# Turning x by the DMA crossbar and placing side work by a table, in a fused attention and maxout kernel

## Chip, cores, metric

One core of one Trainium2 chip. The metric is device microseconds of one execution. A ratio is the mean time of one kernel's fast runs over the mean of the other's fast runs of the same rounds, so it isn't quite the ratio of the medians quoted beside it.

## The reference

Eight batches, eight heads, 576 tokens of 64 numbers. Keys and values are pooled by eight, the softmax attention's output is x (4608 tokens of 512), and a maxout layer follows:

```python
k_p = k.reshape(B, H, Sp, pool, D).mean(axis=3)          # Sp = 72
v_p = v.reshape(B, H, Sp, pool, D).mean(axis=3)
attn = softmax(scale * q @ k_p.T)
x = (attn @ v_p).transpose(0, 2, 1, 3).reshape(B * S, H * D)
h = np.maximum(np.maximum(x @ w1, x @ w2), x @ w3)       # 512 -> 768
out = h @ w_out                                          # 768 -> 512
```

Inputs and output are float32.

## The kernel before

The maxout layer works on blocks of 512 tokens, nine in all. A block has 18 slots of four matmuls `pw` (blocks 0 and 1 do the first half of them in half-size pieces, 27 slots in all) and four slots of six matmuls `po`. While block n runs, the attention of batch n+1 is done between the slots. A batch is 576 tokens, so a block starts 64 tokens further ahead of its batch each time: block 3 needs chunks 0 to 2 of batch 3, block 7 only chunk 0 of batch 7.

The attention gives x with tokens on partitions; the layer needs features there. So each chunk of 128 tokens is turned, by four TensorE transposes into PSUM and a copy:

```python
def turn_x(b, c0, keep, xn, tag, evac=nc.scalar.copy):
    pxt = psp.tile([128, KCH, 128], F16, name="pxt", tag=tag[0], bufs=tag[1])
    for kc in range(KCH):                                 # KCH = 4
        nc.tensor.transpose(pxt[:, kc, :],
            xn[:, kc // 2, 2 * (kc % 2):2 * (kc % 2) + 2, :], identh)
    g0 = S * b + c0
    evac(out=xT[:, :, g0 + keep:g0 + 128], in_=pxt[:, :, keep:128])

TR = ("tr", 1)        # one PSUM buffer for turning q, k and x
```

Side work came from generators, at slots given by a list of counts; loads were issued by GpSimd, each behind the fold (pooling by adds) that freed its buffer:

```python
PLAN = (2, 4, 5, 6, 8, 8, 9, 10, 11, 12, 13, 14, 15, 16, 17, 18, 18, 19, 19, 20,
        20, 21)
for n in range(1, TOK // NB):
    if n + 2 < B:
        fold_k(n + 2, nc.gpsimd)
        if n + 3 < B:
            load_k(n + 3, nc.gpsimd)
        fold_v(n + 2)
        if n + 3 < B:
            load_v(n + 3, nc.gpsimd)
            load_q(n + 3)
    ...                                   # cut: slots of the block, next(nxt)
```

Stores of the output go out on SyncE's queue (all but two small ones at the end).

The softmax here doesn't subtract the row's maximum and nothing guards it: scores larger than these inputs give would overflow.

Of the kernel before, what the change touches and what calls it, by code (L numbers as in the profile page):

```python
# [14 lines left out]
def kernel(  # L15
# [11 lines left out]
    nc = tc.nc  # L27
# [124 lines left out]
    def turn_q(b, n0, n1, evac, tag):  # L152
        if b not in qTs:
            qTs[b] = sb2.tile([128, 2 * NG, 128], BF16, name="qT", tag="qT")
        pqt = psp.tile([128, n1 - n0, 128], BF16, name="pqt", tag=tag[0],
                       bufs=tag[1])
        qf = qbs[b].rearrange("p hp t d -> p (hp t d)")
        for n in range(n0, n1):
            nc.tensor.transpose(pqt[:, n - n0, :], qf[:, 128 * n:128 * n + 128],  # L159
                                ident)  # L160
        evac(out=qTs[b][:, n0:n1, :], in_=pqt)  # L161
# [13 lines left out]
    def turn_k(b):  # L175
        pkt = keys(b, TR)
        for par in range(2):
            fill_kz(b, par, 0, H, pkt, nc.vector.tensor_copy)
# [22 lines left out]
    def new_et(b):  # L201
        ets[b] = sb2.tile([Sp, H, S], F16, name="et", tag="et")

    def scores(b, h):
        psc = psp.tile([128, 1024], F32, name="psc", tag="att", bufs=2)
        score(b, h, psc[:, 0:320], 0, 0, 5)
        score(b, h, psc[:, 320:512], 1, 0, 3)
        score(b, h, psc[:, 512:576], 1, 3, 4)
        exp(ets[b][:, h, :], psc[0:Sp, 0:S])

    def turn_x(b, c0, keep, xn, tag, evac=nc.scalar.copy):
        pxt = psp.tile([128, KCH, 128], F16, name="pxt", tag=tag[0], bufs=tag[1])
        for kc in range(KCH):
            nc.tensor.transpose(  # L214
                pxt[:, kc, :],
# [4 lines that stand above are left out]
    def values(b, c0):  # L220
        pav = psp.tile([128, 2, 512], F32, name="pav", tag="att", bufs=2)
        for h in range(H):
            nc.tensor.matmul(  # L223
                pav[:, h // 4, 65 * (h % 4):65 * (h % 4) + 65],
                ets[b][:, h, c0:c0 + 128], vp_all[:, b, h, :],
                start=True, stop=True)
        pv = pav[:, :, 0:260].rearrange("p g (h e) -> p g h e", e=65)
        rcp = sb3.tile([128, 2, 4], F32, name="rcp", tag="rcp")
        nc.vector.reciprocal(out=rcp, in_=pv[:, :, :, 64])  # L229
        xn = sb3.tile([128, 2, 4, D], F16, name="xn", tag="xn")  # L230
        nc.vector.tensor_tensor(  # L231
            out=xn, in0=pv[:, :, :, 0:D],
            in1=rcp.to_broadcast([128, 2, 4, D]), op=ALU.mult)
        return xn
# [2 lines left out]
    TR = ("tr", 1)  # L237
    PW = ("pw", 3)

    def queries(b):  # L240

        new_et(b)
        for m, (n0, n1) in enumerate(((0, 5), (5, 10), (10, 14), (14, 18))):
            turn_q(b, n0, n1, nc.scalar.copy, TR)
            yield
            if m == (3 if b == 2 else 2):
                turn_k(b)
                yield
        for h in range(H):
            scores(b, h)  # L250
            yield

    def outputs(b, order="v0 v1 x0 v2 x1 v3 x2 v4 x3 x4", tag=TR, evac=nc.scalar.copy):


        xns = {}
        for step in order.split():
            i = int(step[1])
            c0, keep = CHUNKS[i]
            if step[0] == "v":  # L260
                xns[i] = values(b, c0)
            else:
                turn_x(b, c0, keep, xns[i], tag, evac)
            yield

    def hidden_part(n, jc, c0, c1, hT):
        col = slice(NB * n + c0, NB * n + c1)
        t = None
        for wi in range(3):
            pw = psp.tile([128, c1 - c0], F32, name=f"pw{wi}", tag="pw", bufs=3)  # L270
            for kc in range(KCH):
                nc.tensor.matmul(pw, w_sb[wi][:, kc, bass.ts(jc, 128)],  # L272
                                 xT[:, kc, col],
                                 start=(kc == 0), stop=(kc == KCH - 1))
            if wi == 0:
                t = sb2.tile([128, c1 - c0], F16, name="t0", tag="t0")
                nc.scalar.copy(out=t, in_=pw)  # L277
            elif wi == 1:
                t1 = sb2.tile([128, c1 - c0], F16, name="t1", tag="t1")
                nc.vector.tensor_tensor(out=t1, in0=t, in1=pw, op=ALU.max)  # L280
                t = t1
            else:
                nc.vector.tensor_tensor(out=hT[:, jc, c0:c1], in0=t, in1=pw,  # L283
                                        op=ALU.max)
            yield

    def hidden(n, hT):

        halves = n < 2
        if halves:  # L290
            for c0 in (0, NB // 2):
                for jc in range(3):
                    yield from hidden_part(n, jc, c0, c0 + NB // 2, hT)
        for jc in range(3 if halves else 0, JCH):
            yield from hidden_part(n, jc, 0, NB, hT)
# [22 lines left out]
    def new_hT():  # L318
        return sb2.tile([128, JCH, NB], F16, name="hT", tag="hT")
# [4 lines left out]
    def heat(n):  # L324
        for _ in range(n):
# [3 lines left out]
    ATT = ("att", 2)  # L329
    new_kp(0)  # L330
    k16 = const.tile([96, 6, 4, D], F16, name="k16", tag="k16")
    pkp0 = [psp.tile([128, 6, D], F32, name="pkp", tag="pw", bufs=3)
            for _ in range(2)]
    heat(10)

    def add_k0(i):
# [1 line left out]
                                in1=kts[0][:, i:i + 2, 4:8], op=ALU.add)  # L338

    def sum_k0(i):  # L340
        for p in pkp0:
            for j in range(4):
                nc.tensor.matmul(p[:, i:i + 2], identh[0:96, :], k16[:, i:i + 2, j, :],
                                 start=(j == 0), stop=(j == 3))

    def put_k0(i, j):
        nc.vector.tensor_copy(out=kps[0][:, i:j, 0, :], in_=pkp0[0][0:96, i:j])
        nc.scalar.copy(out=kps[0][:, i:j, 1, :], in_=pkp0[1][0:96, i:j])

    add_k0(0)  # L350
    sum_k0(0)
# [45 lines left out]


    nc.vector.memset(kz_all[1], 0.0)
    hT0 = new_hT()  # L400
    out0 = outputs(0, "v2 v3 x2 v4 x3 x4")

    def early():
        pool_k(1, PW)
        yield
        turn_k(1)
        yield
        new_et(1)
        for m, (n0, n1) in enumerate(((0, 5), (5, 10), (10, 14), (14, 18))):
            turn_q(1, n0, n1, nc.vector.tensor_copy, TR)  # L410
            if m > 1:
                scores(1, m - 2)
            yield
        for h in range(2, H, 2):
            scores(1, h)
            scores(1, h + 1)
            yield

    side = early()
    steps = {18: 1, 19: 1, 21: 1, 22: 1, 23: 1, 24: 1, 25: 1, 26: 1}  # L420
    for slot, _ in enumerate(hidden(0, hT0)):
        if slot > 0:
            next(out0, None)
        for _ in range(steps.get(slot, 0)):
            next(side)
        if slot > 24:
            h = 4 * (slot - 25)
            pool_v(1, h, h + 4, TR, nc.scalar.copy)
    out1 = outputs(1, "v0 v1 x0 x1 v2 v3 x2 v4 x3 x4", evac=nc.vector.tensor_copy)
    for mm, _ in enumerate(project(0, hT0)):  # L430
        for _ in range((1, 0, 0, 0)[mm]):
            next(side)
        for _ in range((0, 1, 2, 2)[mm]):
            next(out1)
    side = out1
    fold_k(2, nc.gpsimd)
    load_k(3, nc.gpsimd)
    load_q(3)
# [1 line left out]
    load_v(3, nc.gpsimd)  # L440


    def batch(b):
        yield from queries(b)
        yield from outputs(b, *(("v0 v1 x0 v2 x1 x2 v3 x3 v4 x4",) if b == 2 else ()))


    PLAN = (2, 4, 5, 6, 8, 8, 9, 10, 11, 12, 13, 14, 15, 16, 17, 18, 18, 19, 19, 20,
            20, 21)
    PLAN1 = (9, 11, 13, 15, 19, 20, 21, 22, 23, 24, 25, 26, 26, 27, 28, 28, 29, 29, 30,  # L450
             30)
    for n in range(1, TOK // NB):
        if n + 2 < B:
            fold_k(n + 2, nc.gpsimd)
            if n + 3 < B:
                load_k(n + 3, nc.gpsimd)
            fold_v(n + 2)
            if n + 3 < B:
                load_v(n + 3, nc.gpsimd)
                load_q(n + 3)  # L460
        hT = new_hT()
        nxt = batch(n + 1) if n + 1 < B else iter(())
        plan = PLAN1 if n == 1 else PLAN
        slot = 0
        for part in (hidden(n, hT), project(n, hT)):
            for _ in part:
                if slot < 8:
                    next(side, None)
                for _ in range(plan.count(slot)):
                    next(nxt, None)  # L470
                slot += 1
        side = nxt


# [28 lines left out]
```

## Time and profile before

| | before |
|---|---|
| time, median of 4 | 264.33 us (264.19 to 265.34) |
| span of the profiled run | 262.3 us |
| TensorE / VectorE / ScalarE / GpSimd busy | 95 / 51 / 48 / 45 % |
| steady block (108.21 to 135.03 us) | 26.82 us |

TensorE is the bound, at full clock. In the timeline of an engine each row is a start, a length and a group of instructions; a bracket gives the idle time before it and what ended it. The prediction shows the lines, and how they are read.

```profile
L314 SPq DMA_DIRECT2D out_dram<-osb x5: 467/594/1353, 105.7 to 109.6; - x5
...
DMA to landing us min/median/max: 7.3/9.0/10.6
```

These five stores of 128 KB landed 7 to 11 us after issue, against a median of 2.4 over the kernel: v, q and k were being loaded just then.

### The profile page before, as it was taken

How to read it: one execution, taken by the hardware profiler on the slowest of the kernel's cores; microseconds unless marked ns; L12 is line 12 of the kernel's file. 1: busy time of each engine (PE TensorE's matmuls, PEld its weight loads, DVE VectorE, ACT ScalarE, POOL GpSimd, SP SyncE). 2: the span in 40 equal slices, each digit the busy share in tenths (PEclk: the TensorE clock that was granted, in tenths of full speed). 3: DMA queues.
4: the chain of work that ended last, by engine and by line, in shares of the span. 5: the costliest groups of instructions: out<-in, count | busy, mean ns of one | idle time of the engine just before them, and what ended most of it. 6: DMA issues, size and time to landing. Idle time of an engine off the chain costs nothing.

```text
span 262.3 us, 4747 instructions
## 1 busy us (share of the span) xinstructions
PE 250.3 (95%) x1902; PEld 142.6 (54%) x1902; DVE 132.7 (51%) x243; ACT 125.9 (48%) x225; POOL 117.6 (45%) x84
## 2 busy tenths in 40 slices
PE   7899999988997999999999999999999999999992
PEld 3678556675554555555555555555555554444441
DVE  4567561766344546364635463556446554523430
ACT  1464237243754574548464746464656463132221
POOL 8653000999899999899790896000000000000000
PEclk9999999999999999999999999999999999999998
DMA  7999999886698975987987705100510042015006
GB/s 185 202 197 209 199 234 226 257 202 113 157 238 180 196 182 115 231 266 139 215 239 180 113 4 132 28 2 0 121 42 0 2 110 50 4 41 119 0 12 152
DMA packets 21027, 34.73 MB, mean 132 GB/s; under 512 B 2668, under 2 KB 13548, under 8 KB 20428
## 3 DMA queue, kind: packets, MB, share of 16 engines
q0 software_dynamic: 14048, 21.44, 42.0%
q1 hardware_dynamic: 6796, 12.85, 19.3%
q8 instruction: 15, 0.25, 0.4%
q10 hardware_dynamic: 160, 0.13, 0.2%
q14 instruction: 8, 0.07, 0.1%
HBM read 34.60 MB, written 9.44 MB: 168 GB/s over the span
## 4 chain that ended last, share of the span: by engine, by line
PE 87%; DVE 4%; ACT 4%; issue 1%; DMA 1%; SPq 0%; DVEq 0%
PE pw L272 49%; PE po L305 16%; PE psc L194 6%; PE pav L223 4%; PE pqt L159 3%; PE pxt L214 3%; PE wm L326 2%; ACT xT L218 2%; PE pvp L148 1%; DVE t L280 1%; DMA out_dram<-osb 1%; ACT et L199 1%; DVE xn L231 1%; PE pkt L166 1%; DVE kz L171 1%
## 5 line engine op out<-in xcount | busy, mean ns | idle before, releaser
L272 PE MATMUL pw<-xT,mw 128*128 128x512 f16 (+1 forms) x720 | 158.1, 358 | 0.9 <-ACT xT L218 0.7
L272 PEld LDWEIGHTS <-mw 128*128 128x128 f16 x720 | 64.3, 98 | 48.5 <-issue 0.8
L280 DVE TENSOR_TENSOR t<-t,pw 128x512 f16<-128x512 f16 (+1 forms) x60 | 38.0, 633 | 75.2 <-PE pw L272 46.3
L277 ACT CAST t<-pw 128x512 f16<-128x512 f32 (+1 forms) x60 | 32.6, 543 | 41.6 <-PE pw L272 39.0
L305 PE MATMUL po<-mwo,hT 128*128 128x512 f16 (+1 forms) x222 | 51.5, 373 | 0.0
L199 ACT ACTIVATE et<-psc 72x576 f16<-72x576 f32 (+2 forms) x62 | 40.4, 661 | 16.1 <-PE psc L194 16.1
L283 DVE TENSOR_TENSOR hT<-t,pw 128x512 f16<-128x512 f16 (+1 forms) x60 | 37.9, 632 | 11.0 <-PE pw L272 7.8
L127 POOL TENSOR_TENSOR vt<-vt 72x2048 f32<-72x2048 f32 (+1 forms) x12 | 41.2, 3432 | 4.5 <-DMA vt<-in_v_dram 4.0
L127 POOL TENSOR_TENSOR kt<-kt 96x1536 f32<-96x1536 f32 (+1 forms) x12 | 31.5, 2622 | 23.2 <-DMA kt<-in_k_dram 22.6
L310 ACT COPY osb<-po 128x512 f32<-128x512 f32 (+1 forms) x36 | 20.8, 579 | 38.7 <-PE po L305 38.5
L305 PEld LDWEIGHTS <-hT 128*128 128x128 f16 x222 | 19.9, 97 | 19.4 <-DVE hT L283 1.7
L231 DVE TENSOR_TENSOR xn<-pav,rcp 128x512 f16<-128x512 f32 x40 | 27.6, 691 | 1.4
L194 PE MATMUL psc<-qT,kz 128*128 128x64 bf16 (+3 forms) x192 | 25.6, 246 | 1.2 <-DVE kz L171 1.2
L161 ACT COPY qT<-pqt 128x512 bf16<-128x512 bf16 (+1 forms) x25 | 15.9, 637 | 21.5 <-PE pqt L159 21.5
L194 PEld LDWEIGHTS <-kz 128*128 128x128 bf16 x192 | 17.5, 98 | 15.0 <-DVE kz L171 2.0
L218 ACT COPY xT<-pxt 128x512 f16<-128x512 f16 (+1 forms) x34 | 18.6, 547 | 4.3 <-PE pxt L214 4.2
L223 PEld LDWEIGHTS <-et 72*128 72x128 f16 x320 | 15.2, 98 | 4.6 <-issue 0.5
L223 PE MATMUL pav<-vp,et 72*128 72x65 f16 x320 | 17.2, 194 | 0.4 <-ACT et L199 0.4
L214 PEld LDWEIGHTS <-xn 128*128 128x128 f16 x160 | 11.7, 97 | 10.7 <-DVE xn L231 3.1
L229 DVE RECIPROCAL rcp<-pav 128x8 f32<-128x8 f32 x40 | 8.2, 204 | 18.4 <-PE pav L223 18.3
L214 PE MATMUL pxt<-identh,xn 128*128 128x128 f16 x160 | 15.5, 219 | 2.0 <-DVE xT L218 0.7
L159 PEld LDWEIGHTS <-qb 128*128 128x128 bf16 x144 | 10.0, 97 | 7.9 <-issue 2.4
(43 smaller groups left out, 116.8 us busy)
## 6 DMA issues: line engine op xcount, KB each, us to landing
out_dram<-osb SPq DMA_DIRECT2D x70, 128.0 KB, 2.4
kt<-in_k_dram POOLq DMA_DIRECT2D x5, 1152.0 KB, 8.3
vt<-in_v_dram POOLq DMA_DIRECT2D x5, 1152.0 KB, 10.0
qb<-in_q_dram POOLq DMA_DIRECT2D x7, 576.0 KB, 13.3
mw<-in_moe_w_dram POOLq DMA_DIRECT2D x9, 256.0 KB, 10.0
kt<-in_k_dram SPq DMA_DIRECT2D x3, 384.0 KB, 4.8
kt<-in_k_dram SPq DMA_DIRECT2D x1, 1152.0 KB, 10.0
vt<-in_v_dram SPq DMA_DIRECT2D x1, 1152.0 KB
```

The lines of the kernel that those rows point to most:

```text
L127: e.tensor_tensor(out=t[:, :, 0:n, :], in0=t[:, :, 0:n, :], in1=t[:, :, n:2 * n, :], op=ALU.add)
L194: nc.tensor.matmul(out, kz_all[b % 2][:, f % 2, h, :], qTs[b][:, n + i0:n + i1, 64 * (h % 2):64 * (h % 2) + 64], start=True, stop=True)
L199: nc.scalar.activation(out=out, in_=in_, func=FT.Exp, scale=1.0 / 64.0)
L214: nc.tensor.transpose(pxt[:, kc, :], xn[:, kc // 2, 2 * (kc % 2):2 * (kc % 2) + 2, :], identh)
L218: evac(out=xT[:, :, g0 + keep:g0 + 128], in_=pxt[:, :, keep:128])
L223: nc.tensor.matmul(pav[:, h // 4, 65 * (h % 4):65 * (h % 4) + 65], ets[b][:, h, c0:c0 + 128], vp_all[:, b, h, :], start=True, stop=True)
L231: nc.vector.tensor_tensor(out=xn, in0=pv[:, :, :, 0:D], in1=rcp.to_broadcast([128, 2, 4, D]), op=ALU.mult)
L272: nc.tensor.matmul(pw, w_sb[wi][:, kc, bass.ts(jc, 128)], xT[:, kc, col], start=(kc == 0), stop=(kc == KCH - 1))
L277: nc.scalar.copy(out=t, in_=pw)
L280: nc.vector.tensor_tensor(out=t1, in0=t, in1=pw, op=ALU.max)
L283: nc.vector.tensor_tensor(out=hT[:, jc, c0:c1], in0=t, in1=pw, op=ALU.max)
L305: nc.tensor.matmul(po, hT[:, jc, bass.ts(mm, 128)], wo_sb[:, jc, c], start=(jc == 0), stop=(jc == JCH - 1))
```

## The change

Three intents. x of batches 3 to 7 is turned by a transposing DMA and leaves TensorE. Every step of side work gets its slot from a table, so that single steps can be moved. The loads of k and v wait for the first matmuls of a block and go ahead of the folds, q's load between the folds. Beside this, batch 0's keys are summed once, not twice.

```diff
     def turn_x(b, c0, keep, xn, tag, evac=nc.scalar.copy):
+        if b > 2:
+            g0 = S * b + c0
+            nc.sync.dma_start_transpose(
+                out=xT[:, :, g0 + keep:g0 + 128],
+                in_=xn.rearrange("p g h d -> p (g h d)")[keep:128])
+            return
...
-        xn = sb3.tile([128, 2, 4, D], F16, name="xn", tag="xn")
+        xn = sb3.tile([128, 2, 4, D], F16, name="xn", tag="xn", bufs=6)
...
+    def plan(n):
+        b = n + 1
+        got = {1: [(b, "q0")], 2: [(b, "q1")], 3: [(b, "k")], 5: [(b, "q2 s0")],
+               6: [(b, "s1")], 7: [(b, "q3 s2")]}
+        got.update({5 + h: [(b, f"s{h}")] for h in range(3, H)})
+        got.update({14: [(b, "v0 x0")], 15: [(b, "v1 x1")], 17: [(b, "v2 x2")],
+                    18: [(b, "v3 x3")], 19: [(b, "v4 x4")]})
+        if n == 2:
+            got[1].insert(0, (2, "x4"))
+        return got
+
+    def pool_work(n, mm):        # mm: last matmul of the block's first slot
+        if n + 3 < B:
+            after((load_k(n + 3, nc.gpsimd), load_v(n + 3, nc.gpsimd)), mm)
+        if n + 2 < B:
+            fold_k(n + 2, nc.gpsimd)
+        if n + 3 < B:
+            load_q(n + 3)
+        if n + 2 < B:
+            fold_v(n + 2)
...
-        for p in pkp0:
-            for j in range(4):
-                nc.tensor.matmul(p[:, i:i + 2], identh[0:96, :], k16[:, i:i + 2, j, :],
+        for j in range(4):
+            nc.tensor.matmul(pkp0[:, i:i + 2], identh[0:96, :], k16[:, i:i + 2, j, :],
```

Cut: the tables of blocks 0 and 1, the reading of the table, the removed generators.

## The prediction

> **What bounds the kernel now.** I read the page first: busy shares, slices, chain, groups.
>
> ```profile
> PE 250.3 (95%) x1902; PEld 142.6 (54%) x1902; DVE 132.7 (51%) x243; ACT 125.9 (48%) x225; POOL 117.6 (45%) x84
> ...
> PEclk9999999999999999999999999999999999999998
> ...
> PE 87%; DVE 4%; ACT 4%; issue 1%; DMA 1%; SPq 0%; DVEq 0%
> ...
> L218 ACT COPY xT<-pxt 128x512 f16<-128x512 f16 (+1 forms) x34 | 18.6, 547 | 4.3 <-PE pxt L214 4.2
> ...
> L214 PE MATMUL pxt<-identh,xn 128*128 128x128 f16 x160 | 15.5, 219 | 2.0 <-DVE xT L218 0.7
> ```
>
> TensorE is busy for 95% of the span at full clock, and 87% of the chain is TensorE's. ACT and DVE are at half load, so freeing them is worth nothing by itself; a matmul taken off TensorE, or a stall of TensorE taken away, is worth its own length. The turning of x is 160 of TensorE's 1902 matmuls, 4 for each of 40 chunks. Its mean of 219 ns is a latency, not a cost, because matmuls overlap; for the cost I go to the timeline of PE and read start to start. This is the border between two steady blocks (a block: 18 slots of 4 matmuls `pw`, 4 slots of 6 matmuls `po`, side work in between):
>
> ```profile
> 131.73 1.46 PE L305 MATMUL po<-mwo,hT 128*128 128x512 f16 x6
> 133.03 0.39 PE L214 MATMUL pxt<-identh,xn 128*128 128x128 f16 x4
> 133.25 0.42 PE L223 MATMUL pav<-vp,et 72*128 72x65 f16 x8
> 133.51 1.46 PE L305 MATMUL po<-mwo,hT 128*128 128x512 f16 x6
> 134.81 0.39 PE L214 MATMUL pxt<-identh,xn 128*128 128x128 f16 x4
> 135.03 1.03 PE L272 MATMUL pw<-xT,mw 128*128 128x512 f16 x4
> 136.13 0.38 PE L214 MATMUL pxt<-identh,xn 128*128 128x128 f16 x4
> 136.35 1.89 PE L272 MATMUL pw<-xT,mw 128*128 128x512 f16 x8
> ```
>
> A group of four turns takes 133.25 - 133.03 = 0.22 us. Four `pw` matmuls take 0.865 us elsewhere in this timeline, so the group after 135.03 could start at 135.90 but starts at 136.13: 0.23 us in which TensorE waits for the one "tr" PSUM buffer, which ACT is still copying (L218, 0.59 us). The same gap stands at 109.31, 162.96, 189.79 and 216.61, once for each of batches 3 to 7.
>
> In the timeline of the first blocks the gaps are larger:
>
> ```profile
> 52.49 0.60 PE L272 MATMUL pw<-xT,mw 128*128 128x256 f16 x4
> 53.77 0.38 PE L214 MATMUL pxt<-identh,xn 128*128 128x128 f16 x4 [0.68 <-DVE xT L218]
> ...
> 62.79 1.03 PE L272 MATMUL pw<-xT,mw 128*128 128x512 f16 x4
> 64.21 0.31 PE L194 MATMUL psc<-qT,kz 128*128 128x320 bf16 x1 [0.39 <-DVE kz L171]
> ...
> 78.67 0.42 PE L223 MATMUL pav<-vp,et 72*128 72x65 f16 x8
> 79.77 1.02 PE L272 MATMUL pw<-xT,mw 128*128 128x512 f16 x4 [0.68 <-ACT xT L218]
> ...
> 83.58 0.40 PE L214 MATMUL pxt<-identh,xn 128*128 128x128 f16 x4 [0.57 <-DVE xn L231]
> ```
>
> Each bracket is a step of side work placed one slot too early behind a slower engine: two turns too close (53.77), scores behind the two key copies (64.21), the block's first matmul behind a turn placed in the last slot (79.77), a turn behind its own values (83.58).
>
> **What the Trainium skill says.** "TensorE: Matmul & The Clock Gate", Part 2 (back-to-back issue gap): 55.6 ns for 128 columns when warm. The trace agrees: 0.22 us / 4 = 55 ns. "VectorE: DVE Perf Modes", The three transpose paths: 1309 ns for a 128x128 crossbar transpose by DMA against 390 ns on TensorE. "Advanced Engine Details and Errata", X-Bar Transpose (TRN2): transposing DMAs are as fast as regular ones, and only one transposing stream may be in flight. Here all 25 are on SP's queue, so the second point is met. For the first, no run here has such a transfer yet; the nearest is the output store, also 128 KB on that queue: median 592 ns to issue and 2.4 us to landing, but up to 10.6 us when loads are in flight.
>
> **The change part by part.**
>
> 1. *Turns of batches 3 to 7 leave TensorE.* 5 batches x 5 chunks x 0.22 us = 5.5 us of TensorE, all on the path. The matching 25 ACT copies (some 14 us) are not on it. The "tr" gap goes with them: 5 x 0.23 = 1.15 us. Together 6.7 us.
>
> 2. *Table of steps by slot.* The instruction orders, compared, show which steps moved. Block 0: x4 of batch 0 is one slot later (22.51 to 22.91, 0.4 us), and two slots rather than one lie between pooling and turning k of batch 1 (30.96 to 31.42, 0.46 us). Block 1: x3 and x4 of batch 1 are spread to slots 5 and 7; 52.93 to 53.77 is 0.84 us. x2 of batch 2 turns a slot earlier, so the next block's first matmul should not wait: 78.93 to 79.77, 0.84 us. x4 comes well after its values: 82.85 to 83.58, 0.73 us. That is 3.3 us. Not removed: the wait for x1 at 49.72 (0.43), q0 behind x4 in one slot (83.80 to 84.44, 0.64). The key copies (two of 0.755 us, "tr" held throughout) now sit amid half-size slots of 0.44 us and will stop q2 rather than the scores: about 1.0 us in place of the 1.2 around 64.21. I take 0.2. Sum 3.5 us.
>
> 3. *Batch 0's keys are summed once.* 12 matmuls fewer in the first 10 us. At 107 ns each for the first four (0.85 us for 8) and 55 after, the groups end earlier by 0.43, 0.22 and 0.22 us. Against this DVE writes both halves: 512 and 256 columns in place of 256 and 128, by its row's slope of 0.13 us per 128 columns 0.26 and 0.13 us more. As the groups wait partly on DMA and DVE, I take 0.3 us.
>
> 4. *25 transposing DMAs.* 3.2 MB on engines that are nearly idle after 160 us (DMA 0.17 of the time, 40 GB/s). They cost only if a block's first matmul waits for one. Batch b's first chunks serve block b, which starts at token 512b while the batch starts at 576b; block 3 needs chunks 0 to 2 of batch 3, blocks 4 and 5 two chunks, 6 and 7 one. Batch 3 is tight: its v2 follows slot 17, DVE has hT (0.69) ahead of the reciprocal and xn (0.9), so SP gets x2 some 1.6 us after v2, while TensorE has 4 x 1.30 + 2 x 0.26 = 5.7 us left. About 4 us remain for the transfer. I estimate 3 to 4 us (2.4 of a store, a little more for the turn), with q's load of batch 5 beside it. I set 0.7 us for this block, nothing for the others.
>
> 5. *Loads tied to the first matmul.* k and v of batch n+3 start with block n, ahead of the folds; POOL folds k and v in 16 us of a 25 us block and a fold is needed a block later. Worth nothing, costs nothing; it keeps two large loads away from the turns.
>
> Sum: 6.7 + 3.5 + 0.3 - 0.7 = 9.8 us. I take off 0.6 for small new stalls among the moved steps, so 9.2, and 264.3 - 9.2 gives **255.1 us**.
>
> **Rivals.**
>
> - *The transposes are slow and become the wait.* If each takes 5 us and they go one after another, x2 of batch 3 lands some 8 us late, and block 4 waits about 3 us as well: 266 us or more. At 3 us each in a row, only block 3 waits some 3 us: 257.5 us. For it: 1309 ns for a single 128x128 is not negligible, and a 128x512 chunk is four of these (5.2 us if they simply add). Against it: the stores' 2.4 us, 16 engines, and the slack that grows by 64 tokens a block.
> - *TensorE doesn't get shorter, because something else has the pace of a block.* ACT has 15.4 us and DVE 14.0 us in a 26.8 us block; after the change ACT has some 12.5. Against this rival: neither is near. It would leave only the early gaps: about 260 us.
> - *The new table trades gaps for gaps.* Slots 14 to 19 now hold five values steps closer together, and DVE must do hT before the projection can end. By my count hT of the last part is ready 0.4 us before its matmul. If that fails, 0.3 us a block, 1.5 us in all: 256.6 us.
>
> **Range and chances.** If all gaps close and the turns are hidden: 264.3 - 11 = 253. With 3 us of waiting for the crossbar and half the early gaps left: 259. So 252.5 to 259.0, more of the risk above. The 2% border is 259.0; only the slow-transpose rival or two failures together reach it. Faster 0.87, same 0.10, slower 0.03.
>
> **What would show it.** Right: PE matmul count down by 112, to some 1790; L214 on PE with x60; steady blocks 25.4 us against 26.8; no gap after a block's first slot; transposes landing within 4 us; span some 253. Wrong: a bracket naming DMA xT on the first `pw` of block 3 (or of several blocks), brackets with DVE hT on `po`, or new brackets on L159 behind L171. The prediction fails most surely if the transposes land after 5 us or more or hold each other up.

## The result

255.97 us, median of 4 runs (254.78 to 256.55), against 264.33: the ratio is 0.967 (0.9627 to 0.9713). Executions over 1.5% slower than the fastest of the same kernel are left out of the means. The prediction said 255.1 with a range of 252.5 to 259.0. The page of the changed kernel, and from the view of its DMAs the line of the transposing ones (count, then median us from issue to landing):

```profile
span 253.9 us, 4576 instructions
...
PE 242.0 (95%) x1790; PEld 135.6 (53%) x1790; DVE 131.5 (52%) x239; ACT 115.4 (45%) x202; POOL 117.8 (46%) x84
...
PE 81%; DMA 11%; POOL 2%; DVE 2%; issue 2%; ACT 1%; POOLq 0%; DVEq 0%; ACTq 0%
```

```profile
xT<-xn SPq DMA_TRANSPOSE x25, 2.6
```

TensorE has 112 matmuls fewer and is still the bound, with a granted clock of 1.0 in this run. The DMAs have come into the chain: two loads at the start, and the crossbar once. The timeline of PE, at the places that answer to those shown of before:

```profile
23.43 4.53 PE L280 MATMUL pw<-xT,mw 128*128 128x256 f16 x40
28.45 1.47 PE L185 MATMUL pkp<-kt,identh 96*128 96x384 f16 x8 [0.49 <-DMA kt<-in_k_dram]
...
53.55 0.39 PE L220 MATMUL pxt<-identh,xn 128*128 128x128 f16 x4
...
60.35 0.40 PE L159 MATMUL pqt<-ident,qb 128*128 128x128 bf16 x4 [0.88 <-DVE kz L171]
...
78.65 0.39 PE L220 MATMUL pxt<-identh,xn 128*128 128x128 f16 x4
78.87 1.89 PE L280 MATMUL pw<-xT,mw 128*128 128x512 f16 x8
80.60 0.39 PE L220 MATMUL pxt<-identh,xn 128*128 128x128 f16 x4
81.44 0.44 PE L159 MATMUL pqt<-ident,qb 128*128 128x128 bf16 x5 [0.46 <-ACT xT L224]
...
102.62 2.75 PE L314 MATMUL po<-mwo,hT 128*128 128x512 f16 x12
105.96 1.89 PE L280 MATMUL pw<-xT,mw 128*128 128x512 f16 x8 [0.59 <-DMA xT<-xn]
...
128.86 2.75 PE L314 MATMUL po<-mwo,hT 128*128 128x512 f16 x12
131.45 1.89 PE L280 MATMUL pw<-xT,mw 128*128 128x512 f16 x8
```

The brackets at 53.77, 79.77 and 83.58 of before are gone, and steady blocks meet without a gap (128.86 + 12 x 0.216 = 131.45). From the first hidden matmul at 18.20 us on, six brackets stand in the whole timeline: a load at 28.45, the key copies at 34.03 (0.39) and 60.35, x1 of batch 1 at 50.18 (0.25; before 0.26), x4 at 81.44, and at 105.96 x2 of batch 3. Start to start, part by part, from the two timelines:

| part | before us | after us | difference |
|---|---|---|---|
| start and block 0, up to its first `po` | 42.38 | 42.85 | +0.47 |
| from there to block 1 | 7.34 | 7.33 | -0.01 |
| block 1 | 30.05 | 28.69 | -1.36 |
| block 2 | 28.44 | 27.09 | -1.35 |
| blocks 3 to 6 | 107.29 | 101.98 | -5.31 |
| blocks 7 and 8, up to the last block's `po` | 36.72 | 36.26 | -0.46 |
| last `po` to the end | 10.1 | 9.7 | -0.4 |

The sum is -8.4, the difference of the spans. Block 2's number is itself a sum: four turns of batch 3 (0.89 us) and one gap (0.73) left, two steps moved to block 1 (0.48), and the crossbar's wait (0.75) came. In the last row the chain of waits has an output store whose buffer VectorE needs again: 2.8 us of waiting before and 2.0 after. Whether the change did that is not shown.

### The profile page after: what moved, and what is told of

Read it like the earlier page. It is cut to its first block, busy times and chain, and to the rows that moved or that the text cites. A ratio compares the mean times of both kernels' runs of the same rounds, so it can differ in the third digit from the quotient of the medians.

```text
span 253.9 us, 4576 instructions
## 1 busy us (share of the span) xinstructions
PE 242.0 (95%) x1790; PEld 135.6 (53%) x1790; DVE 131.5 (52%) x239; ACT 115.4 (45%) x202; POOL 117.8 (46%) x84
## 4 chain that ended last, share of the span: by engine, by line
PE 81%; DMA 11%; POOL 2%; DVE 2%; issue 2%; ACT 1%; POOLq 0%; DVEq 0%; ACTq 0%
PE pw L280 50%; PE po L314 16%; PE psc L194 5%; DMA kt<-in_k_dram 5%; DMA mw<-in_moe_w_dram 4%; PE pav L229 3%; PE pqt L159 3%; DMA xT<-xn 2%; PE pxt L220 1%; POOL vt L77 1%; DMA out_dram<-osb 1%; DVE t L289 1%; PE pvp L148 1%; DVE kz L171 1%; PE pkt L166 1%
## 5 line engine op out<-in xcount | busy, mean ns | idle before, releaser
L314 PE MATMUL po<-mwo,hT 128*128 128x512 f16 (+1 forms) x222 | 50.7, 373 | 0.0
L292 DVE TENSOR_TENSOR hT<-t,pw 128x512 f16<-128x512 f16 (+1 forms) x60 | 38.0, 634 | 14.0 <-PE pw L280 10.1
L159 PE MATMUL pqt<-ident,qb 128*128 128x128 bf16 x144 | 13.0, 219 | 1.8 <-DVE kz L171 1.3
L171 DVE COPY kz<-pkt 64x576 bf16<-64x576 bf16 (+1 forms) x16 | 11.4, 715 | 4.4 <-PE pkt L166 4.3
L130 POOL TENSOR_TENSOR kp<-kt 96x384 bf16<-96x384 f32 x12 | 11.7, 993 | 0.5
```

The source lines that it names most:

```text
L159: nc.tensor.transpose(pqt[:, n - n0, :], qf[:, 128 * n:128 * n + 128], ident)
L292: nc.vector.tensor_tensor(out=hT[:, jc, c0:c1], in0=t, in1=pw, op=ALU.max)
L314: nc.tensor.matmul(po, hT[:, jc, bass.ts(mm, 128)], wo_sb[:, jc, c], start=(jc == 0), stop=(jc == JCH - 1))
```

## The experiments

The theory after the result: TensorE's 5.5 us and the small gap of each block are the gain; the table gives some 2.5 us in blocks 1 and 2, and nothing in block 0, because loads rule there; the ties of the loads are worth nothing, as predicted; x2 of batch 3 is late because q and v are being loaded. Rivals: the table alone gave the gain; the crossbar's transfers queue behind each other. All kernels gave correct results. Twelve were run.

**The changed kernel again.**

> The changed kernel once more, as the base for the runs beside it. Both theories: 255 to 256.5 us, 0.967 of before. First pooling matmul of batch 1's keys starts at its load's landing (28.4 us), first pooling matmul of batch 0's values at its load's landing (12.2 us), first matmul of block 3 held some 0.75 us by the crossbar.

Measured: 255.57 us (255.12 to 256.19), ratio 0.9674 (0.9658 to 0.9691). It is the base for the three kernels of its rounds (table without the crossbar, loads in before's order, loads of batch 5 late); the others are compared through their ratios to before. Block 3 was held again, with a bracket of 0.46 us.

**Table without the crossbar.** The branch is taken out, turns stand a slot or more after their values:

```diff
-        if b > 2: ...
-        got.update({14: [(b, "v0 x0")], 15: [(b, "v1 x1")], 17: [(b, "v2 x2")], ...
+        got.update({14: [(b, "v0")], 15: [(b, "v1")], 16: [(b, "x0")], 17: [(b, "x1 v2")],
+                    18: [(b, "v3")], 19: [(b, "x2 v4")], 20: [(b, "x3")], 21: [(b, "x4")]})
```

> New table, loads and key sums, but every x turned on TensorE, a slot or more after its values. Theory (the crossbar gives 25 x 0.22 us of TensorE time and takes back 0.75 us at block 3): 4.8 us over the changed kernel, 260.8 us, L-line of the turns at x160, steady blocks 26.6 us. Rival (the table gave the gain, the crossbar is a wash): within 1 us of the changed kernel.

Measured: 261.43 us (261.16 to 262.75), ratio 0.9904; 5.9 us over the changed kernel of the same rounds, where 4.8 was expected. The first matmuls of two blocks:

```profile
133.02 1.89 PE L274 MATMUL pw<-xT,mw 128*128 128x512 f16 x8
...
159.64 1.89 PE L274 MATMUL pw<-xT,mw 128*128 128x512 f16 x8
```

A steady block is 26.62 us, 1.1 us (five groups of 0.22) over the changed kernel's 25.5. So the turns were the larger part, and the rest of the change without the crossbar is worth 1%. The rival falls.

**Crossbar without the table.** The kernel before, with only the branch in `turn_x` and six buffers for xn.

> Kernel before with only the crossbar branch and six xn buffers. Theory (the crossbar saves 6.7 us of TensorE time, but with before's order x2 goes out behind the stores of the block's third projection, and beside loads of k, v and q that are issued whenever a fold ends; a transpose beside them lands in 12 to 15 us, as the two runs with moved loads showed): block 3 held 8 us or more, blocks 4 and 5 held too; 268 to 280 us, slower than before. Rival (the crossbar is hidden anyhow): 257.6 us.

Measured: 307.66 us (293.40 to 310.75), slower by 11% in its fastest run. The other three runs, 306.89 to 310.75, are over 1.5% above it; they were not traced. Direction as expected, size far beyond it. Waits of TensorE in the profiled run, the fastest: total us, times, longest.

```profile
PE pw L278 <- DMA xT<-xn: 16.0, 1, 16.0
PE pw L278 <- DMA out_dram<-osb: 11.0, 1, 11.0
PE pw L278 <- issue: 3.2, 1, 3.2
```

And its granted clock in 40 slices:

```profile
PEclk9999999999999996579996699979999999999999
```

Blocks 3, 4 and 5 are held 16, 11 and 3 us. (The name behind each arrow is inferred.) The granted clock fell as well: it was 0.50 from 115 to 128 us, over 4 us past the end of the first wait, and 0.53 and 0.57 in some 4 us after the other two. So the crossbar by itself, in before's order, is a loss. What makes it a gain is in the rest of the change.

**Loads in before's order.** In the changed kernel, each load behind the fold that frees its buffer, no tie.

```diff
-            after((load_k(n + 3, nc.gpsimd), load_v(n + 3, nc.gpsimd)), mm)
+            (fold_k, load_k, fold_v, load_v, load_q, as in the kernel before)
```

> Changed kernel with the loads of k, v and q as before: each behind the fold that frees its buffer, no tie to a block's first matmul. Theory (the ties are worth nothing): within 0.5 us of the changed kernel, block 3 still held 0.3 to 1.5 us by x2. Rival (the ties keep the loads away from the crossbar): transposes of batch 3 land in 6 us or more and block 3 is held 2 us or more, 257.5 us or more.

Measured: 266.64 us (265.88 to 275.09), ratio 1.0078 (the two runs over 270 us count as slow): 11 us over the changed kernel, and 0.8% over before. My theory that the ties are worth nothing fell. In the profiled run GpSimd issues v of batch 5 at 98.6 and q at 99.4; x0 went out ahead of them at 97.9 and landed in 2.5 us, x1 at 99.2 took 11.4, x2 at 101.0 took 12.2:

```profile
113.32 3.57 PE L280 MATMUL pw<-xT,mw 128*128 128x512 f16 x8 [7.97 <-DMA xT<-xn]
```

The eight matmuls took 3.57 us instead of 1.89: the granted clock was 0.50 from 113.3 to 117 us, so the loss is larger than the wait. Stores issued in the same stretch (98 to 114 us) had a median of 12.9 us. So it isn't the transposing that is slow: what goes out on SyncE's queue just behind bulk loads lands late, as in the kernel before. The crossbar turned a latency that nobody waited for into one that a block's first matmul waits for.

Beside the run above, this kernel has the same order of loads, but the new table (and the single sum of keys): 266.6 us against 293.4 in that one's fastest run. There x0 went out at 104.8 us and landed 11.0 us later; here it went out at 97.9. So with the crossbar in, the table is worth some 27 us, some ten times what it gives with all turns on TensorE (2.5 us). The earlier turns are the likely reason; they weren't tested by themselves.

**Loads of batch 5 late.** They are issued after block 2's last hidden part, meant to stay out of x2's way. (They are left out at the start of that block.)

```diff
+                if slot == 17 and n == 2:
+                    after((load_k(5, nc.gpsimd), load_v(5, nc.gpsimd)), mms[-1])
+                    load_q(5)
```

> Changed kernel with the loads of batch 5 issued after the last hidden part of block 2, that is behind v2 and beside only the end of x2. Theory (x2 lands late, 4.8 us against a median of 2.6, because k, v and q are being loaded): x2 lands in 3.5 us or less, no gap at the first matmul of block 3, 0.7 us less than the changed kernel. Rival (x2 is late because three transposes queue up behind each other): the gap of 0.75 us stays, time unchanged.

Measured: 267.89 us (267.40 to 268.25), a miss: I had put the loads at 99.6 to 101 us, right beside x2 at 100.8, which landed 14.8 us later; block 3 was held 10.5 us. It measures the same as the run above, from the other side: x0, which went out at 97.7 us ahead of the loads, landed in 2.5 us.

**Order of loads kept, tie removed.**

```diff
-            after((load_k(n + 3, nc.gpsimd), load_v(n + 3, nc.gpsimd)), mm)
+            load_k(n + 3, nc.gpsimd)
+            load_v(n + 3, nc.gpsimd)
```

> Changed kernel with the new order of loads and folds but without the wait of k's and v's loads for a block's first matmul. Theory (the tie is what matters: without it GpSimd issues k and v of batch 6 as soon as it has folded v of batch 4, near 98.8 us, right beside x2 of batch 3): x2 lands in 10 us or more, block 3 is held 6 us or more, 262 to 267 us. Rival (the order of loads before folds matters, the tie doesn't): 256 us.

Measured: 281.28 us (279.44 to 283.60), ratio 1.0656. GpSimd ran ahead and issued k of batch 6 at 98.0 and v at 98.6 us, as expected; x0, x1 and x2 landed in 16.3 to 17.8 us. The size of the loss was more than I had expected:

```profile
117.27 3.57 PE L280 MATMUL pw<-xT,mw 128*128 128x512 f16 x8 [12.10 <-DMA xT<-xn]
...
153.00 3.57 PE L280 MATMUL pw<-xT,mw 128*128 128x512 f16 x8 [8.17 <-issue]
```

Block 4 is held as well, and from 105 to 117 us the mean granted clock was 0.61, from 117 to 124 us 0.70. So the tie alone is worth 25 us here. GpSimd had been ahead of TensorE; the tie is a brake that puts two 1152 KB loads at the start of a block, where no transpose is.

**q of batch 5 a block later.** In the changed kernel two bulk transfers are still in flight when x2 goes out at 101.0 us: v of batch 5 (landing at 101.4) and q (at 104.5).

```diff
-        if n + 3 < B:
+        if n + 3 < B and n != 2:
             load_q(n + 3)
+        if n == 3:
+            after((load_q(5),), mm)          # at block 3's first slot, ahead of k and v
```

Cut, here and in the next one: `load_q` returns its DMA, so that it can be tied.

> Changed kernel with only the load of q of batch 5 moved from the middle of block 2 to block 3's first matmul. Theory (x2 lands 4.8 us after its issue because v of batch 5, landing at 101 us, and q, landing at 104 us, are in flight; without q v lands earlier too, and an undisturbed transpose lands in 2.5 us): x2 lands in 2.5 to 3.5 us, block 3 isn't held, 0.7 us less than the changed kernel, 254.9 us. Rival (three transposes in a row queue up behind each other): x2 still lands near 4.8 us and the time stays.

Measured: 255.27 us, fast runs 254.77 to 255.36, ratio 0.9659 (0.9643 to 0.9675), not clear of the changed kernel's. The fifth run, which was profiled, took 263.08. Up to block 3 its trace answers the question: x0, x1 and x2 landed in 3.5, 2.5 and 2.4 us and block 3 wasn't held. Transposes in a row do not queue up; the loads are the cause. In that run block 4 was held 5.6 us, so what is moved away from one batch may hit the next; this run alone doesn't show that it did.

**Every q from batch 5 on a block later.**

```diff
-        if n + 3 < B:
-            load_q(n + 3)
+        if n == 1:
+            load_q(4)
+        # and at a block's first slot, ahead of k and v:
+        if n > 2 and n + 2 < B:
+            after((load_q(n + 2),), mm)
```

> Changed kernel with each load of q from batch 5 on moved from the middle of a block to the first matmul of the next block, ahead of that block's k and v. Theory (bulk loads beside a transpose delay it): block 3 is no longer held (0.7 us less, 254.9 us) and all loads of a block are over some 20 us into it, so blocks 4 and on aren't held either. Rival (what is moved away from batch 3 collides with batch 4, as in one run of the kernel with a late q): block 4 is held some us in some or all runs; 256 to 263 us.

Measured: 255.02 us (254.83 to 255.41, five runs), ratio 0.9654 (0.9642 to 0.9667). The transposes issued from 99 to 102 us:

```profile
xT<-xn SPq DMA_TRANSPOSE x3, 2.4
```

against 6.1 in the changed kernel in the same stretch. No block is held by the crossbar in its trace. The gain over the changed kernel is some 0.5 us by the ratios (0.9674 to 0.9654), expected 0.7, hardly clear of noise in time, plain in the trace.

**Batch 0's keys summed twice again.**

> Changed kernel with batch 0's keys summed twice again, 12 matmuls more in the first 10 us. Theory (the start waits for the load of batch 0's values, which lands at 12.1 us, so matmuls ahead of it cost nothing): first pooling matmul of the values at 12.0 to 12.3 us, first matmul of the hidden layer at 18.0 to 18.2 us, time within 0.3 us of the changed kernel. Rival (my prediction): 0.3 us more, at the first matmul of the hidden layer too.

Measured: 256.32 us (255.90 to 256.79), ratio 0.970. The time is 0.7 us worse by the ratio (0.9674 in other rounds, the intervals overlap), but not at the start: values' first pooling matmul at 12.12 us (after 12.23 in the changed kernel), first hidden matmul at 18.08 (18.20). The changed kernel's first scores had come earlier (10.49 us, 10.96 in the kernel before) and then it waited longer for the load of v:

```profile
12.12 1.03 PE L148 MATMUL pvp<-vt,identh 72*128 72x256 f16 x8 [0.24 <-DMA vt<-in_v_dram]
```

So the 12 matmuls were beside a load. What made this run slower stands in its trace later: keys of batch 1 landed at 29.1 us instead of 28.4, and block 3 was held 1.0 us. Whether the edit has to do with either is open.

**Keys of batch 1 loaded ahead of the last third of the weights.**

```diff
     for i in range(3):
+        if i == 2:
+            load_k(1, nc.gpsimd, F16)
         load_w(slice(256 * i, 256 * i + 256))
-    load_k(1, nc.gpsimd, F16)
```

> Changed kernel with the load of batch 1's keys issued ahead of the last third of the weights. Theory (the pooling of batch 1's keys, one slot earlier in the new table, waits for this load): it starts without a wait, near 27.8 us instead of 28.4 us; 0.6 us less if the weights are in time, 255.0 us. Rival (the load isn't the limit, or the weights now are): a wait of the same size moves to the weights at slot 21; time unchanged.

Measured: the wait is gone in the trace (pooling at 27.62 us behind matmuls that end there) and no weight is late. In time it is inconclusive: two runs of 254.6 and 254.8 us, four of 257.5 to 258.5 (two of these count as slow), ratio 0.9698 (0.9652 to 0.9744). The profiled run was the quickest; what the others waited for isn't shown, but their mean granted clock was 0.990 to 0.993, against 0.999 in the two quick ones.

**Key copies on two engines.** The second copy of `kz` for batches 1 and 2 goes to ScalarE.

```diff
-            fill_kz(b, par, 0, H, pkt, nc.vector.tensor_copy)
+            fill_kz(b, par, 0, H, pkt, nc.scalar.copy if par and b < 3
+                    else nc.vector.tensor_copy)
```

> Changed kernel with the second of the two key copies of batches 1 and 2 on ScalarE instead of VectorE. Theory (the single turning buffer is held by two copies in a row of 0.755 us on VectorE, and the next turn of q waits for both): the gaps before the turns of q behind L171 (0.55 us near 34, 1.04 us near 60) shrink to 0.3 us or less each; 1.0 us less than the changed kernel, about 254.6 us. Rival (the gaps only move on, to scores or to ScalarE's exponentials): within 0.3 us of the changed kernel.

Measured: 256.05 us (254.74 to 258.62), ratio 0.9677; a miss. The brackets before the turns of q went from 0.39 to 0.19 us and from 0.88 to 0.76; 0.3 or less was expected of both. The copies did not run side by side: VectorE's ended at 32.72 us and ScalarE's began at 32.76, each time one behind the other. Two engines writing halves of one tile were kept in order here. In this profiled run block 3 was held 2.2 us, with x2 landing in 6.4.

**Shifted q, early keys and split copies together, and q0 a slot behind x4 in block 2.**

> The three edits of this call together, and in block 2 each step up to the last score one slot later, so that q's first turn isn't right behind the turn of x4. Theory: 1.0 + 0.6 + 0.7 us of the three, and 0.6 us of the gap at 81.4 us; 252.7 us. Rival: gaps move on and half of it stays, 254.2 us; or block 4 is held by the crossbar, 256 us or more.

Measured: 253.48 us (253.29 to 253.53), ratio 0.9592 (0.958 to 0.9605): the best kernel here, 0.8% below the changed one. In its trace the waits for the load at 28 us, for x4 at 81 and for the crossbar at 105 are gone; those for the key copies and for x1 at 49 remain. It lies between its theory (252.7) and its rival (254.2), about the middle, which fits the key copies' failure.

How long block 3 was held differs from run to run of nearly one kernel: brackets of 0.59, 0.46, 1.01, 2.20 and 0.31 us in the profiled runs of the changed kernel, its repeat, the two sums, the split copies and the early keys. The two kernels that keep q away from x2 in every block have the narrowest times, spreads of 0.6 and 0.2 us over all their runs, against 0.9 to 3.9 in those five. That this wait is what spreads the times is possible, not shown: only one run of each was traced, and the table without the crossbar, which has no such wait, spread by 1.6 us.

## Why the prediction was right

The total was 0.9 us too low and the mechanism right; where it goes wrong, terms of about a microsecond cancel, and one judgement was wrong that the total didn't depend on. Of its own signs, the count of matmuls (1790), the steady block (25.5 us) and the span (253.9) came; "landing within 4 us" did not: x0 to x2 of batch 3 took 7.0, 6.1 and 4.8 us, and the slowest of all 8.4.

1. *Turns leave TensorE, 6.7 us.* Right. 21 of the 25 turns and all five gaps lie in blocks 3 to 7: 21 x 0.222 + 5 x 0.23 = 5.8 us. Measured there: 5.31 + 0.46 = 5.8 us. The table without the crossbar gave the same from the other side: 26.62 against 25.5 us a block.

2. *The table, 3.5 us.* Right in blocks 1 and 2: gaps of 0.84, 0.84 and 0.73 us went, the wait of 1.04 us for the key copies came, as said, onto q2, and q0 behind x4 stayed (0.62 us). That the table is worth some ten times more once x goes by DMA (266.6 us against 293.4) was not seen. Wrong in block 0: I booked 0.86 us and nothing came. Both gaps that I named went (0.40 and 0.46 us), but pooling had been moved a slot earlier onto the landing of its load (27.78 to 28.45, 0.67 us lost), and the key copies hold q's first turn longer (33.48 to 34.03, 0.41 us more than before). Before, the load had landed just ahead of its use and left no bracket.

3. *Keys summed once, 0.3 us.* Wrong: nothing at the start, where it was booked (the time of the kernel with two sums leaves 0.7 us unexplained). The first scores came 0.5 us earlier, then TensorE waited for v's load: its pooling started at 11.9 to 12.2 us in the five traces in which I looked it up. In the changed kernel the bracket there names ScalarE, but v landed 8.2 us after its issue at 3.9 us, just before the start at 12.23. The first hidden matmul was even 0.25 us later than before (18.20, 17.95), which with block 0's terms makes the +0.47 of the table. "The groups wait partly on DMA and DVE" was the right thought with too small a discount.

4. *Crossbar, 0.7 us at block 3, else nothing.* Right in size: 0.75 us between 105.21 and 105.96. Partly luck: with its own 4 us of slack and 3 to 4 us for the transfer nothing would have waited; the 0.7 was a margin. x2 landed in 4.8 us beside loads, and an undisturbed one in 2.4, so neither the little more for the turn nor the rival's 5.2 us for four transposes in a row came. The chain of waits puts it in one line:

```profile
101.00 4.83 DMA xT<-xn
```

5. *"Worth nothing, costs nothing" of the tied loads.* This is the step that failed. The sentence after it ("it keeps two large loads away from the turns") named the very mechanism and gave it no number. Without the tie the kernel takes 281.3 us, with before's order of loads 266.6. The total was right only because the tie was part of the change. I had seen "up to 10.6 us when loads are in flight" in before's stores and still took the median of 2.4: the rival of slow transposes was weighed by the cost of a transfer alone, not by what else was on the DMA engines at that moment.

6. *0.6 us for new small stalls.* Blocks 3 to 6 have none beside the 0.75 us; the stalls sit in block 0, where the sum of points 2 and 3 fell short by 1.6 us (1.16 booked, 0.47 lost). The 0.4 us at the end have no term.

## What to carry to other kernels

When a transfer takes work off the bound engine, ask first who now waits for its landing, and then what else is on the DMA engines between its issue and that wait; a median landing says little about it, the landings of other transfers in that window do. A producer that runs ahead (GpSimd here) may issue its loads at the worst moment; a tie to the consumer's progress cost nothing that these traces show and was worth 25 us here, three times the gain of the whole change. Matmuls removed from in front of a load, or a step moved up to its load's landing, gained nothing, and a load that landed just in time left no bracket in the trace to warn of it.

## What the Trainium skill lacked or had wrong

- "DMA: Bandwidth & Descriptors", Rules for kernel authors, says that a transpose next to ordinary DMAs needs nothing. The row is about corrupted results, and there all runs agree, each correct; it lacks the time: 2.4 to 2.6 us to landing undisturbed, 5.5 to 18 us when k, v or q loads of 576 to 1152 KB were issued just before or beside it.
- "Advanced Engine Details and Errata", X-Bar Transpose (TRN2), says that transposing DMAs are as fast as regular ones. The runs agree on landing (a chunk of 128x512 in 2.4 us beside a store's 2.4 from 160 us on; 12.2 beside 12.9 when loads are in flight), but no page gives the issue time of such a transpose, SBUF to SBUF on trn2: SyncE took 1.2 us for one, 0.6 for a store.
- No page has how long a SyncE transfer waits behind GpSimd's bulk loads: 7 to 11 us for stores in the kernel before.
